# Row-paired first transform stage, full-array second stage, and a complex product summed in PSUM, in a convolution and gated-unit kernel

## The chip, the core and the metric

The kernel runs on one core of one Trainium2 chip, as one program. Its engines are TensorE (PE in the profile, with PEld for the loading of its stationary operand), VectorE (DVE), ScalarE (ACT), GpSimd (POOL) and SyncE (SP), which issues nearly all DMAs. Operands lie in the on-chip memory SBUF; matmul results go to PSUM, which here is cut into eight tiles of 128 partitions by 512 floats (eight banks). The metric is the device time of one execution in microseconds, lower is better.

## What is computed

For an input `u` of 2048 tokens by 448 channels the reference mixes two branches with a gate per token. Branch A is a diagonal state-space convolution: from 448 x 256 modes it makes a kernel of 2048 taps per channel and convolves by a Fourier transform of twice the length. Branch B is a gated linear unit with 1792 hidden units.

```python
    def _A_ref(u, log_A_real, A_imag, C_real, C_imag, log_dt, D_skip):
        ...
        P = jnp.exp((A * dt[:, None])[:, :, None] * pos[None, None, :])
        K = 2.0 * jnp.einsum("dn,dnl->dl", C, P).real
        ...
        Kf = jnp.fft.rfft(K, L2)
        Uf = jnp.fft.rfft(u_t, L2)
        y = jnp.fft.irfft(Uf * Kf[None, :, :], L2)[:, :, :L]
        ...
        return y + u * D_skip[None, None, :]

    def _B_ref(x, w_gate, w_up, w_down):
        g = jnp.einsum("bsd,df->bsf", x, w_gate)
        u = jnp.einsum("bsd,df->bsf", x, w_up)
        h = _sigmoid(g) * u
        return jnp.einsum("bsf,fd->bsd", h, w_down)

    x = A_u
    g = _sigmoid((x * gate_w).sum(-1, keepdims=True))
    a = _A_ref(x, ...)
    b = _B_ref(x, B_w_gate, B_w_up, B_w_down)
    return g * a + (1 - g) * b
```

## The kernel before, in words

**Four kinds of work.** (1) *Parameters*: phases and powers of the modes, on VectorE, ScalarE and GpSimd. (2) *Kernel generation*, 28 chunks of 16 channels (`kgen`): TensorE makes phases in the tiles `tp` (L827, L842), ScalarE takes sines and cosines, VectorE multiplies them by powers (L866, L881 to L885), and 32-column matmuls (L890) sum over the modes into `kp`; the taps collect in `ke` and go to `kd` in DRAM, one store after chunk 13 and one after chunk 27. (3) The *gated unit*: for each of 14 hidden tiles and each block of 512 tokens two sums of 11 matmuls, the gate's and the up branch's, each in a PSUM tile `gu` (L995 to L1000; weights and inputs are split into a high and a low part, and the last 64 rows of the contraction have a matmul of their own, L1000). ScalarE takes the tanh of the gate's sum (L983), VectorE multiplies by the up branch's sum (L984) and splits the result (L987), and three matmuls per tile (L1012 to L1014) add to the output in `dn`, which VectorE adds to `ob` (L1028). (4) The *transforms*.

**The transforms.** The channels are cut into two halves of 224 (`HD`). A `Chain` holds one half's data in a tile `fx` of 128 partitions by 32 columns by 224 channels, and works in place. There are four chains: `u` of both halves, whose spectra are stored to `us`, and the generated kernel of both halves. The steps:

- *Stage 1* (L442 in `stage1_pair`): the data comes as 64 rows by 32 columns; each column has its own 64 x 128 matrix (real and imaginary parts of 64 rows side by side), loaded in tiles `ft` of four matrices. A pair of columns is two plain float32 matmuls of 224 columns into one PSUM tile `fps`, which ScalarE writes back to `fx` (L369). The profile shows each float32 matmul as two records. The fourth chain (the kernel's second half) takes another way, `stage1_split`: its data is loaded twice, to both row halves; ScalarE and VectorE make a rounded and a remainder part `sp` (L426, L427), and four single-pass matmuls per pair (L432, L433) use matrices `sh` and `sl` that GpSimd's queue loads (L321).
- *Transposition*: through DRAM (`shf`) by SP's DMAs for three chains, on VectorE (L453) for the fourth.
- *Stage 2* (L471 in `spectrum_pair`): for each pair of columns four float32 matmuls with 64 output columns each, so that the column pair lies on the two partition halves, and real and imaginary parts lie side by side.
- *Product* (`product_pair`): `ua`, 229 KB of `us`, comes by DMA. VectorE forms all four real products in `ub` (L500), then two subtractions and two additions on 64 partitions each (L506, L507). One float32 matmul of 448 columns takes the inverse second stage into `fz` (L511), and ScalarE writes it back.
- *Back*: transposition again, then `back_j`: float32 matmuls with 64 output columns (L546), and VectorE adds the result, times the gate, to the gated unit's part (L550).

**What sets the order.** Every instruction is recorded with what it reads and writes, a cost and a priority. `Plan.order` is a list scheduler: it takes the engine that can start first and on it the ready instruction of the lowest priority number, with its own cost formulas (`c_mm`, `c_dve`, ...). The resulting order is fixed; on the chip each engine runs its list in order and waits on semaphores. Generation has priority 20, the `u` chains 30, the kernel's chains 40 and 41, the gated unit's matmuls 60, so those fill what the others leave. A tile from a pool needs a free buffer, and the counts are constants: `GUB` for `gu`, `FPS` for `fps`, `SX` and `SK` for the buffers of the kernel's two chains.

**PSUM before.** `gu` 3, `dn` 1, `fps` 1 and, during generation, `tp` 2 and `kp` 1: eight. After generation the latter three give way to `fps`, `fz` and `fzx` of the last stage.

## Time and profile before

| | |
|---|---|
| times of the runs | 881.62, 883.9, 888.26 us |
| median | 883.9 us |
| span of the profiled execution, first to last instruction | 878.0 us |
| mean granted TensorE clock | 0.972 |
| HBM read and written | 78.32 MB and 36.24 MB |

The profile gives the profiled execution's span, and no time of its own that includes what lies around it; the median of the runs is 5.9 us above that span.

How to read it: "busy" is the time in which at least one instruction of the engine ran. Matmuls are pipelined and their ends are modelled, so that a record's length holds some 0.2 us in which the next matmul already runs; the distance between the starts of two neighbours is what one matmul costs. A row of groups gives line, engine, operation, tile written and tiles read, form, count, then busy us and mean ns, then the engine's idle time before them and what ended it. A row of waits gives who waited for whom: us in total, times, longest.

### The profile page before, as it was taken

What the parts mean: (1) busy time and instruction counts of PE and PEld (TensorE: products, weight loads), DVE (VectorE), ACT (ScalarE), POOL (GpSimd) and SP (SyncE); (2) the same over time, 40 slices, a digit from 0 to 9 for tenths busy, and PEclk for the clock granted to TensorE, in tenths of its full rate; (3) what the DMA queues carried; (4) which work ended last, traced back from release to release, by engine and by line L of the source; (5) the groups of instructions that cost most, each with busy time, mean ns of one, the idle gap of its engine ahead of it and who ended that gap; (6) DMA issues with size and microseconds to landing.
All of it is one profiled execution on the core that took longest, in us unless ns stands there. A gap on an engine that the chain in (4) does not pass through costs nothing. (4 is left out here: it accounts for less than half of the span.)

```text
span 878.0 us, 16776 instructions
## 1 busy us (share of the span) xinstructions
PE 808.5 (92%) x6688; PEld 541.5 (62%) x6688; DVE 733.0 (83%) x982; ACT 501.3 (57%) x862; POOL 330.1 (38%) x358
## 2 busy tenths in 40 slices
PE   4988799999988999999998999999989999889987
PEld 2665576666655667776665666666766566445543
DVE  2869984798995999999897989899846788978995
ACT  3544654677766877777677987777722352221210
POOL 3367644454452645374355535645021120000000
PEclk9989999899997999999999999999999999998999
DMA  9951377222290326436494116422959953294324
GB/s 242 226 107 32 97 216 168 95 95 93 81 194 26 125 83 146 160 116 157 135 219 120 44 60 180 125 84 79 208 104 248 280 153 109 70 212 119 85 56 117
DMA packets 95831, 115.66 MB, mean 132 GB/s; under 512 B 31465, under 2 KB 80937, under 8 KB 95241
## 3 DMA queue, kind: packets, MB, share of 16 engines
q1 hardware_dynamic: 93704, 110.98, 48.4%
q0 software_dynamic: 2048, 3.61, 1.6%
q8 instruction: 53, 0.87, 0.4%
q14 instruction: 26, 0.20, 0.1%
HBM read 78.32 MB, written 36.24 MB: 130 GB/s over the span
## 5 line engine op out<-in xcount | busy, mean ns | idle before, releaser
L995 PE MATMUL gu_gps<-xs_glu,wh_glu 128*128 128x512 f32 x336 | 148.0, 440 | 11.7 <-ACT wh_glu L969 11.6
L866 DVE TENSOR_TENSOR es_eg<-tb_eg 128x512 f32<-128x512 f32 x168 | 125.5, 772 | 20.7 <-PE kp_egp L890 19.2
L997 PE MATMUL gu_gps<-xs_glu,wl_glu 128*128 128x512 f32 x336 | 135.3, 403 | 1.2 <-POOL wl_glu L971 1.2
L996 PE MATMUL gu_gps<-xs_glu,wh_glu 128*128 128x512 f32 x336 | 135.5, 403 | 0.0
L1012 PE MATMUL dn_gps<-vh_glu,hh_glu 128*128 128x448 f32 x224 | 98.6, 440 | 7.0 <-ACT ob_glu L1021 3.5
L971 POOL TENSOR_TENSOR wl_glu<-xr_glu,wh_glu 128x512 fp32r<-128x512 f32 x44 | 77.8, 1777 | 65.7 <-ACT wh_glu L969 65.7
L995 PEld LDWEIGHTS gu_gps<-xs_glu,wh_glu 128*128 128x128 f32 x336 | 65.6, 195 | 41.2 <-issue 19.0
L1013 PE MATMUL dn_gps<-vh_glu,hl_glu 128*128 128x448 f32 x224 | 83.7, 374 | 4.5 <-DVE hl_glu L987 4.5
L1014 PE MATMUL dn_gps<-vl_glu,hh_glu 128*128 128x448 f32 x224 | 83.6, 373 | 0.5 <-POOL vl_glu L971 0.5
L884 DVE TENSOR_TENSOR ec_eg<-ec_eg,es_eg 128x1024 f32<-128x1024 f32 x56 | 79.8, 1426 | 0.0
L997 PEld LDWEIGHTS gu_gps<-xs_glu,wl_glu 128*128 128x128 f32 x336 | 65.3, 194 | 18.0 <-POOL wl_glu L971 2.8
L813 POOL TENSOR_TENSOR tb_eg<-tb_eg 128x96 f32<-128x96 f32 (+2 forms) x84 | 73.4, 877 | 5.8
L827 PE MATMUL tp_egp<-pos_sb,ph_eg 96*128 96x512 f32 x168 | 72.5, 446 | 1.9 <-ACT fr_eg L845 1.7
L885 DVE TENSOR_TENSOR es_eg<-fr_eg,es_eg 128x1024 f32<-128x1024 f32 x56 | 73.3, 1310 | 0.3
L996 PEld LDWEIGHTS gu_gps<-xs_glu,wh_glu 128*128 128x128 f32 x336 | 65.8, 196 | 10.0 <-issue 1.3
L971 POOL TENSOR_TENSOR vl_glu<-vr_glu,vh_glu 128x448 fp32r<-128x448 f32 x24 | 35.5, 1477 | 87.0 <-ACT vh_glu L969 85.5
L1012 PEld LDWEIGHTS dn_gps<-vh_glu,hh_glu 128*128 128x128 f32 x224 | 42.9, 191 | 39.0 <-issue 17.1
L803 POOL MEMSET tb_eg<- 128x96 f32 x28 | 7.8, 283 | 152.0 <-DVE es_eg L866 152.0
L1028 DVE SCALAR_TENSOR_TENSOR ob_glu<-dn_gps,og,ob_glu 128x448 f32<-128x448 f32 x72 | 49.1, 681 | 18.4 <-PE dn_gps L1014 17.7
L859 ACT ACTIVATE ec_eg<-ec_eg,half_pi 128x1024 f32<-128x1024 f32 x56 | 63.9, 1140 | 0.0
L471 PE MATMUL fps_fups<-fx_fu,m_sb 128*64 128x224 f32 x384 | 48.7, 376 | 15.6 <-DMA fx_fu<-shf 7.8
L984 DVE SCALAR_TENSOR_TENSOR sg_glu<-sg_glu,gu_gps 128x512 f32<-128x512 f32 x56 | 38.1, 682 | 24.8 <-PE gu_gps L1000 18.1
(167 smaller groups left out, 1720.0 us busy)
## 6 DMA issues: line engine op xcount, KB each, us to landing
shf<-fx_fu SPq DMA_DIRECT2D x16, 896.0 KB
fx_fu<-shf SPq DMA_DIRECT2D x16, 896.0 KB
xr_glu<-in_w_dram SPq DMA_DIRECT2D x52, 256.0 KB
us<-fx_fu SPq DMA_DIRECT2D x4, 1792.0 KB
vr_glu<-in_w_dram SPq DMA_DIRECT2D x28, 224.0 KB
gt_pro<-in_u_dram SPq DMA_DIRECT2D x8, 448.0 KB
fx_fu<-in_u_dram SPq DMA_DIRECT2D x8, 448.0 KB
kd<-ke_eg SPq DMA_DIRECT2D x8, 448.0 KB
```

Of the source, the lines that this page charges most:

```text
L813: pool(96 * m, lambda n=n, m=m: G.tensor_mul(g3(n + 1, m), g3(1, m), g3(n, 1).to_broadcast([128, 32, 3, m])))
L827: T.matmul(tp.real, ph[:, c % 2, 128 * nh:128 * nh + 128].bitcast(F32R), pos[:, 512 * i:512 * i + 512], start=True, stop=last)
L866: V.tensor_mul(o.rearrange("p d (i k) -> p d i k", k=ny), x.unsqueeze(3).to_broadcast([128, 16, nx, ny]), y.unsqueeze(2).to_broadcast([128 ...
L884: op("DVE", c_dve(1024), lambda: V.tensor_mul(ec[:, :, 0:64], ec[:, :, 0:64], es[:, :, 0:64]), [es], [ec], prio)
L885: op("DVE", c_dve(1024), lambda: V.tensor_mul(es[:, :, 0:64], fr.real, es[:, :, 0:64]), [fr], [es], prio)
L971: op(eng, cost(n), lambda: e.tensor_sub(view(l), a(), view(h).bitcast(F32)), [res, (h, key)], [(l, key)], prio)
L995: T.matmul(p.real, wh[:, k, cs], x[:, k], start=(k == 0), stop=False)
L996: T.matmul(p.real, wh[:, k, cs], x[:, 4 + k], start=False, stop=False)
L997: T.matmul(p.real, wl[:, k, cs], x[:, k], start=False, stop=False)
L1012: T.matmul(p[:, :D], hh[:, ts], vh.real, start=(i == 0), stop=False)
L1013: T.matmul(p[:, :D], hl[:, ts], vh.real, start=False, stop=False)
L1014: T.matmul(p[:, :D], hh[:, ts], vl.real, start=False, stop=(i == len(fs) - 1))
```

## The change

Stage 1 of all chains works on both row halves of the array. Even columns of the data lie on partitions 0 to 63, odd ones on 64 to 127, and so do the matrices. Four columns are four float32 matmuls, which alternate between the row halves and write two PSUM tiles. `stage1_split` and its casts, `sh`, `sl` and `sp` are gone; the fourth chain loads its data once.

Stage 2 is one float32 matmul of 448 columns with the whole 128 x 128 matrix, so that real parts lie on the lower partitions and imaginary parts on the upper ones. For the product `ua` is loaded in two arrangements side by side (the real parts of `us` on both partition halves, then the imaginary parts on both), 458 KB by two DMAs. VectorE's product is one instruction as before. The four subtractions and additions are gone: the inverse is two float32 matmuls of 448 columns that accumulate in one PSUM tile, the second with a rearranged, sign-changed copy of the matrix, which widens `m_sb` to 384 columns.

The buffers: `GUB` 3 to 2, `FPS` 1 to 2; `fz` and `fzx` are gone, the first half's later steps stay in the two `fps` tiles, and the second half's chain has three `fps` tiles of its own; `ua` 3 to 2, `ub` 1 to 2. The planner can give one instruction two new tiles of one tag.

```diff
-WB, ECB, FRB, TPB, KPB, GUB, FPS, SGB, XRB = 3, 2, 2, 2, 1, 3, 1, 3, 5
+WB, ECB, FRB, TPB, KPB, GUB, FPS, SGB, XRB = 3, 2, 2, 2, 1, 2, 2, 3, 5
...
-SX = {'ft': 1, 'ua': 3, 'ub': 1, 'fps': 1, 'fz': 1}
-SK = {'ft': 2, 'sh': 2, 'sl': 2, 'sp': 3, 'ua': 3, 'ub': 1, 'fps': 1, 'fz': 1}
+SX = {'ft': 1, 'ua': 2, 'ub': 2, 'fps': 2}
+SK = {'ft': 2, 'ua': 2, 'ub': 2, 'fps': 3}
...
+    m[0:64, 256:384], m[64:128, 256:384] = m[64:128, 128:256], -m[0:64, 128:256]
...
+    s1 = s1.reshape(64, 16, 2, 128).transpose(2, 0, 1, 3).reshape(128, 16 * 128)
...
-            t = o["ready"]
+            t, n = o["ready"], {}
...
-                if q["next"] != x.idx or not q["free"]:
+                k = n[id(q)] = n.get(id(q), -1) + 1
+                if q["next"] + k != x.idx or len(q["free"]) <= k:
                     return None
-                t = max(t, min(q["free"]))
+                t = max(t, sorted(q["free"])[k])
...
-            return self.ps[k].tile(("fps", "fz" + self.suffix)[k], self.bufs[("fps", "fz")[k]], (128, 512))
+            return self.ps[k].tile("fps", self.bufs["fps"], (128, 512))
...
-        def stage1_pair(self, tb, r, l):
-            p = self.psum()
-
-            def f():
-                for i in range(2):
-                    T.matmul(p[:, i * HD:i * HD + HD], tb[0:64, l + i], self.x[0:64, 2 * r + i], start=True, stop=True)
-            op("PE", c_mm(HD, 8), f, [tb, (self.x, r)], [p], self.prio)
-            evac(lambda: self.pair(r), p, [(self.x, r)], self.prio)
+        def stage1_four(self, tb, b, l):
+            x, ps = self.x, [self.psum(), self.psum()]
+            xr = [(x, (z, r)) for z in range(2) for r in (2 * b, 2 * b + 1)]
+            def f():
+                for a in range(2):
+                    for z in range(2):
+                        rows = slice(64 * z, 64 * z + 64)
+                        T.matmul(ps[z][:, a * HD:a * HD + HD], tb[rows, l + a], x[rows, 4 * b + 2 * a + z], start=True, stop=True)
+            op("PE", 2 * c_mm(HD, 4) + 290, f, [tb, *xr], ps, self.prio)
+            for z in range(2):
+                op("Act", c_act(D), lambda z=z: S.activation(
+                    x[:, 4 * b + z:4 * b + z + 3:2], ps[z][:, :D].rearrange("p (a d) -> p a d", a=2), AF.Copy),
+                   [ps[z]], [*xr, (x, 2 * b), (x, 2 * b + 1)], self.prio)
...
-            def f():
-                for c in range(2):
-                    for i in range(2):
-                        T.matmul(p[64 * i:64 * i + 64, c * HD:c * HD + HD], m_sb[:, 64 * c:64 * c + 64],
-                                 self.x[:, 2 * r + i], start=True, stop=True)
-            op("PE", c_mm(HD, 8) + 100, f,
+            op("PE", c_mm(D, 4), lambda: T.matmul(p[:, :D], m_sb[:, 0:128], self.pair(r), start=True, stop=True),
...
-                ua = self.tile("ua", (128, 2, HD))
-                dma(lambda ua=ua, r=r: ua.real, lambda r=r: us[:, 2 * r:2 * r + 2], 128 * 2 * HD * 4,
-                    [(us, r // 8)], [ua], self.prio)
+                ua = self.tile("ua", (128, 2, 2, HD))
+                for c in range(2):
+                    dma(lambda ua=ua, c=c: ua[64 * c:64 * c + 64],
+                        lambda r=r: us.v("(c p) k d -> p c k d", c=2)[:, :, 2 * r:2 * r + 2], 64 * 4 * HD * 4,
+                        [(us, r // 8)], [(ua, c)], self.prio)
...
-            op("DVE", c_dve(2 * D), lambda: V.tensor_mul(      # Ur Kr, Ur Ki, Ui Kr, Ui Ki
-                ub.real, ua.real.unsqueeze(2).to_broadcast([128, 2, 2, HD]),
-                p[:, :D].rearrange("p (c d) -> p c d", c=2).unsqueeze(1).to_broadcast([128, 2, 2, HD])), [ua, p], [ub], prio)
-
-            def add(i):
-                rows = slice(64 * i, 64 * i + 64)
-                V.tensor_sub(x[0:64, 2 * r + i], ub[rows, 0, 0], ub[rows, 1, 1])
-                V.tensor_add(x[64:128, 2 * r + i], ub[rows, 0, 1], ub[rows, 1, 0])
-            for i in range(2):
-                op("DVE", 2 * c_dve(HD), lambda i=i: add(i), [ub], [(x, r)], prio)
+            op("DVE", c_dve(2 * D), lambda: V.tensor_mul(
+                ub.real, ua.v("p c k d -> p c (k d)"), p[:, :D].unsqueeze(1).to_broadcast([128, 2, D])), [ua, p], [ub], prio)
             z = self.psum(1)
-            op("PE", c_mm(D, 4), lambda: T.matmul(z[:, :D], m_sb[:, 128:256], self.pair(r), start=True, stop=True),
-               [(x, r), m_sb], [z], prio)
+            def f():
+                for c in range(2):
+                    T.matmul(z[:, :D], m_sb[:, 128 + 128 * c:256 + 128 * c], ub[:, c], start=c == 0, stop=c == 1)
+            op("PE", c_mm(D, 8), f, [ub, m_sb], [z], prio)
...
-    su = dict(SU, fps=1)
+    su = dict(SU, fps=FPS)
...
-    ks = [Chain(fu, fups, su, 0, P_K, K0D), Chain(fk, fkps, SK, 1, P_K + PKD, True, True)]
+    ks = [Chain(fu, fups, su, 0, P_K, K0D), Chain(fk, fkps, SK, 1, P_K + PKD, True)]
...
-            ks[h].move(fk, fkps, SX)
+            ks[h].move(fk, (fups, fups), SX)
```

60 lines of the change are left out of this document (18 added, 42 removed).

## The prediction

> **What bounds the kernel now.** I read the page's busy times first, then the windows cut at the first and last generation matmul (164.5 and 645.4 us), then the waits in the last two.
>
> ```profile
> span 878.0 us, 16776 instructions
> PE 808.5 (92%) x6688; PEld 541.5 (62%) x6688; DVE 733.0 (83%) x982; ACT 501.3 (57%) x862; POOL 330.1 (38%) x358
> 0.00:164.50 164.50, 135.42 (x485) 95.67 (x485) 120.11 (x158) 80.47 (x127) 88.30 (x67) 0.92 0.64 151
> 164.50:645.40 480.90, 462.69 (x5249) 318.53 (x5248) 433.93 (x538) 362.94 (x628) 228.17 (x272) 0.99 0.43 119
> 645.40:878.00 232.60, 210.36 (x959) 127.30 (x956) 179.00 (x287) 57.90 (x107) 13.60 (x20) 0.98 0.57 144
> ```
>
> A window's row gives its length, the busy us of PE, PEld, DVE, ACT and POOL, the granted clock, the DMA engines' share and GB/s. TensorE is the fullest engine in both long stages (96% and 90%), VectorE second (90% and 77%). The start has neither full; its parameters have their own chain, which the change leaves alone, so I give it nothing. The waits tell how the two engines hold each other:
>
> ```profile
> DVE es_eg L866 <- PE kp_egp L890: 19.2, 19, 3.0
> PE fps_fups L546 <- DMA fx_fu<-shf: 5.3, 1, 5.3
> PE fps_fups L471 <- DVE ubx_fk L500: 4.5, 3, 2.1
> PE dn_gps L1012 <- DVE ob_glu L1028: 2.6, 8, 0.7
> PE fzx_fkps L511 <- DVE fx_fu L507: 1.4, 1, 1.4
> DVE ub_fk L500 <- DMA ua_fk<-us: 7.1, 1, 7.1
> DVE ubx_fk L500 <- DMA uax_fk<-us: 5.6, 3, 2.1
> ```
>
> The first row is generation, the others the last stage. In generation VectorE waits for TensorE's sums; in the last stage TensorE waits 8.5 us for VectorE (4.5 + 2.6 + 1.4), and each waits for DMAs.
>
> **The change part by part.** The prices:
>
> ```profile
> L442 PE MATMUL fps_fups<-fx_fu,ft_fu 64*128 64x224 f32 x192 | 49.3, 377 | 5.2 <-DMA ft_fu<-in_s1t_dram 4.3 <-DMA fx_fu<-kd 0.7
> L471 PE MATMUL fps_fups<-fx_fu,m_sb 128*64 128x224 f32 x384 | 48.7, 376 | 15.6 <-DMA fx_fu<-shf 7.8 <-DVE ubx_fk L500 4.5 <-DMA ph_eg<-phd 3.2
> L471 PE MATMUL fps_fkps<-fx_fk,m_sb 128*64 128x224 f32 x128 | 15.5, 363 | 0.9 <-DVE fx_fk L453 0.9
> L506 DVE TENSOR_TENSOR fx_fu<-ubx_fk 64x224 f32<-64x224 f32 x32 | 13.0, 406 | 0.5
> L507 DVE TENSOR_TENSOR fx_fu<-ubx_fk 64x224 f32<-64x224 f32 x32 | 12.4, 387 | 0.4
> L507 DVE TENSOR_TENSOR fx_fk<-ub_fk 64x224 f32<-64x224 f32 x32 | 12.4, 387 | 0.4
> L506 DVE TENSOR_TENSOR fx_fk<-ub_fk 64x224 f32<-64x224 f32 x32 | 12.3, 383 | 0.6
> L427 DVE TENSOR_TENSOR sp_fk<-fx_fk,sp_fk 64x448 fp32r<-64x448 f32 x16 | 9.9, 622 | 3.5 <-ACT sp_fk L426 3.4
> L984 DVE SCALAR_TENSOR_TENSOR sg_glu<-sg_glu,gu_gps 128x512 f32<-128x512 f32 x56 | 38.1, 682 | 24.8 <-PE gu_gps L1000 18.1 <-ACT wh_glu L969 6.4
> 701.19 0.37 PE L432 MATMUL fps_fkps<-sp_fk,sh_fk 128*128 128x224 f32 x1
> ...
> 702.38 0.47 PE L1012 MATMUL dn_gps<-vh_glu,hh_glu 128*128 128x448 f32 x1
> 801.84 0.36 PE L1014 MATMUL dn_gps<-vl_glu,hh_glu 128*128 128x448 f32 x1
> 802.13 0.98 PE L471 MATMUL fps_fkps<-fx_fk,m_sb 128*64 128x224 f32 x8
> 803.03 0.47 PE L1012 MATMUL dn_gps<-vh_glu,hh_glu 128*128 128x448 f32 x1
> 824.26 0.20 PE dn_gps L1012
> 826.41 0.23 PE gu_gps L995
> 827.78 0.77 PE fz_fkps L511 x2
> ```
>
> *Stage 1, three chains.* A pair is four records: 49.3 us over 48 pairs, 1.03 us each. Four columns cost 2.06 now. Nothing in this trace runs two row halves at once. Its bounds: as two pairs one after the other (2.06, no gain), or as stage 2 does with two column halves: 64.2 us over 64 pairs, 1.00 us for four matmuls of the same 224 columns. I take 1.00, the row of the same shape, as all that differs is which side of the array is halved. That is 24 x 1.06 = 25 us less.
> The Trainium skill, "TensorEngine Tiling (Array Packing)", Key Properties, says that different tiles load and multiply in parallel, row tiles included; by it the sum is the one with 1.00, and without it the gain is zero. The trace agrees for column tiles (1.00 for four against 2.06); no run here shows rows.
>
> *Stage 1, fourth chain.* From 701.19 to 702.38 a pair of four single-pass matmuls takes 1.19 us; 16 pairs 19.0. Eight groups at 1.00 make 8.0 (16.5 at 2.06): 11 us less. VectorE loses L427's 9.9 us.
>
> *Stage 2.* From 802.13 to 803.03 it takes 0.90, and its predecessor L1014 0.29 (801.84 to 802.13) against the 0.20 of an undisturbed down matmul: 0.99. The new matmul has the shape of L511, 0.77: 0.22 less, 64 times, 14 us. Here the same section of the Trainium skill says that changing the tiling mode drains the array; the 0.09 of L1014 fits that, and by the rule alone the full-array form wins on both sides.
>
> *Product.* One more matmul of L511's shape, 32 x 0.77 = 24.6 us more, all in the last stage. VectorE loses L506 and L507, 50.1 us (13.0 + 12.4 + 12.4 + 12.3).
>
> So TensorE is 26 us lighter (25 + 11 + 14 - 24.6) and VectorE 60. *DMAs*: `ua` doubles, 32 x 229 KB = 7.3 MB more on SP, two issues for one, with two buffers for three. SP waits in order, so a `ua` load behind a busy buffer holds back the weights and `acc` loads after it. The fourth chain's data and matrices fall by 1.8 and about 2 MB. The last stage's 0.57 share leaves room on average; the price is between nothing and the two `ua` waits again, 12.7 us. I take nothing: a shorter VectorE turn frees `ua` earlier relative to its next use.
>
> *Where it lies.* The order of the two built programs tells what moved. Of 1232 gate and up matmuls 969 stood before generation's last matmul and 991 do now; of 672 down matmuls 483 and 489. In generation itself TensorE gets 55 and 9 more of them, for 33 and 3 fewer at the start. Generation: 46 pairs of stage 1 become 22 groups (-25.4), 33 second stages (-7.3), 55 x 0.23 + 9 x 0.20 of gated unit (+14.5): -18 us on TensorE. But VectorE, at 434 of 481 us, gets about five more instructions like L984 (+3.4), and only the 19.2 us that it waited for L890 can shrink, so the stage gains between 0 and 15. I take 6, below the middle, because VectorE's work sets its floor. Last stage: fourth chain -11, 31 second stages -6.8, products +24.6, gated unit -22 x 0.23 - 6 x 0.20 = -6.3: TensorE's work is unchanged (+0.5). What goes there are its 8.5 us of waits for VectorE, which falls from 179 to about 118 us; the wait for `shf` (5.3) stays. I take 8. Sum: 878.0 - 6 - 8 = 864 us span; with 5.9 for what lies between this span and the median, **870 us**. One bound is left out of this sum and stands below: the lost `gu` buffer, between 0 and 26.7 us, taken as 0, since the planner knows of two buffers and puts other matmuls between.
>
> **The rivals.**
>
> *1. The gated unit stalls for PSUM (slower).* With three `gu` tiles the next gate sum never needs the last product L984; with two, the next up sum does.
>
> ```profile
> 19.77 0.50 PE L1000 MATMUL gu_gps<-xs_glu,wl_glu 64*128 64x512 f32 x1
> 25.29 0.49 PE L1000 MATMUL gu_gps<-xs_glu,wl_glu 64*128 64x512 f32 x1
> 25.60 0.68 DVE L984 SCALAR_TENSOR_TENSOR sg_glu<-sg_glu,gu_gps 128x512 f32<-128x512 f32 x1
> ...
> 834.47 0.49 PE L1000 MATMUL gu_gps<-xs_glu,wl_glu 64*128 64x512 f32 x1
> 839.64 0.50 PE L1000 MATMUL gu_gps<-xs_glu,wl_glu 64*128 64x512 f32 x1
> 841.14 3.60 DVE L453 STREAM_TRANSPOSE fx_fk<-fx_fk 128x1792 f32<-128x1792 f32 x1
> 845.44 0.77 DVE L984 SCALAR_TENSOR_TENSOR sg_glu<-sg_glu,gu_gps 128x512 f32<-128x512 f32 x1
> ```
>
> The up sum was complete at 834.96, the next gate sum at 840.14, yet L984 ended at 846.21, behind the transposes: 6.1 us in which an up sum in two tiles would stand still, and everything behind it in TensorE's list. Nine of the 56 blocks were late so, first and last shown, by 0.3 to 6.3 us, 26.7 together. It decides if the list places the next sum as tightly as before: 870 + 26.7 = 897 us. Against it: VectorE's queue is shorter in the last stage. For it: generation's long VectorE instructions are untouched, and six of the nine lie there.
> The Trainium skill, "TensorEngine Tiling (Array Packing)", Gotcha 1: PSUM Pressure, says that row tiles must write different banks; so the groups of four take two `fps` tiles, and this is what took the third `gu` tile.
>
> *2. The row halves do not overlap.* Groups of four cost 2.06. Generation's TensorE sum is then +7 (14.5 - 7.3), the last stage gets 2.5 instead of 11 from the fourth chain: +8.5, which eats the 8. With half of the 7 reaching the end, 878 + 3.5 + 0.5 + 5.9 = 888 us, no change.
>
> *3. TensorE's relief passes in full.* Generation gains its 15, and in the last stage the first half's product ends early enough that the `shf` wait (5.3) and the `ua` waits fall under gated-unit work: 8.5 + 5.3, about 14. 878 - 15 - 14 + 5.9 = 855 us. Against it: VectorE's 90% in generation.
>
> **How the numbers follow.** About 1% (8.8 us) is what a measurement can tell from no change: faster is below 875.1, slower above 892.7. Forecast 0.52, its own range 859 to 881; rival 1 0.22; rival 2 0.13; rival 3 0.13. Faster: three quarters of the forecast and rival 3, 0.52 in all. Same: the rest of the forecast (0.13), rival 2 nearly whole (0.12) and half-sized stalls of rival 1 (0.05): 0.30. Slower: 0.18, nearly all rival 1. For 8 in 10 the range runs from 852, which leaves out under half of rival 3, to 899, past the centre of rival 1.
>
> **What would show it.** In the changed kernel's groups: stage 1 with 96 + 32 matmuls in about 1.0 us per four (right) or 2 us (rival 2), starts in pairs a few ns apart; stage 2 at about 0.77; two inverse matmuls at 1.5 us per pair; no VectorE rows but one product per pair. In the windows: the last generation matmul near 639 us, and a last stage near 225 us with VectorE below 125. TensorE's waits should have few rows on VectorE; rival 1 shows as rows of gate or up matmuls waiting for L984 or the tanh, 20 us and more, rival 3 as a generation stage under 470 us. The forecast is wrong if the product's VectorE instruction waits for `ua` by more than the old 12.7 us.

## The result and the profile after

The changed kernel takes **896.6 us** (median of 4, 895.9 to 898.9) against 882.8 us for the kernel before on the same chip: a ratio of **1.0149**, 95% interval 1.0102 to 1.0195. It is slower by about 1.5%, and the forecast was 870. The profiled execution has a span of 894.2 us against 878.0. The profiled execution of the kernel before is one of its faster ones (granted clock 0.972 and span 878.0 us, where 92 other executions have a mean clock of 0.964 and a median span of 880.7), so that up to 7 us (0.008 of 880) of what looks lost to the clock since can be that draw.

The first lines of the page, and then the three windows, cut as for the kernel before at the first and the last generation matmul (155.5 and 655.0 us here; length, then busy us of PE, PEld, DVE, ACT and POOL, granted clock, share of the DMA engines, GB/s):

```profile
span 894.2 us, 15983 instructions
PE 795.5 (89%) x6368; PEld 534.7 (60%) x6368; DVE 679.2 (76%) x838; ACT 492.0 (55%) x846; POOL 320.7 (36%) x342
```

```profile
0.00:155.50 155.50, 123.75 (x460) 88.20 (x463) 117.24 (x154) 76.22 (x122) 74.31 (x59) 0.92 0.61 156
155.50:655.00 499.50, 459.73 (x5108) 316.41 (x5107) 443.27 (x544) 368.22 (x638) 245.30 (x282) 0.96 0.42 118
655.00:894.20 239.20, 212.02 (x810) 130.09 (x806) 118.67 (x141) 47.61 (x87) 1.13 (x1) 0.93 0.61 151
```

TensorE is busy for 13 us less (808.5 to 795.5) and VectorE for 54 less (733.0 to 679.2), and yet generation got 18.6 us longer (480.9 to 499.5) and the last stage 6.6 (232.6 to 239.2); only the start is 9.0 shorter, with 33 gate and up matmuls fewer in it. The granted clock fell in both long stages: 0.99 to 0.96 and 0.98 to 0.93. Against the forecast, generation ends 15.6 us late (655.0 for 639.4) and the last stage is 14.6 too long (239.2 for 224.6).

The groups of the changed operations (busy us, mean ns, idle time before them):

```profile
L450 PE MATMUL fps_fups<-fx_fu,m_sb 128*128 128x448 f32 x96 | 49.3, 611 | 17.2 <-DMA fx_fu<-shf 10.6 <-DMA xr_glu<-in_w_dram 6.5
...
L487 PE MATMUL fps_fkps<-ub_fk,m_sb 128*128 128x448 f32 x64 | 27.2, 547 | 0.0
L422 PE MATMUL fps_fups<-fx_fu,ft_fu 64*128 64x224 f32 x192 | 25.9, 377 | 1.8 <-DMA ft_fu<-in_s1t_dram 1.5 <-DMA fx_fu<-kd 0.2
```

Stage 1 of the three chains is 25.9 us for 24 groups of four, 1.08 us each. One such group of the fourth chain in the timeline, behind a second stage (start, length, number of records):

```profile
700.50 0.92 PE L450 MATMUL fps_fups<-fx_fu,m_sb 128*128 128x448 f32 x2
701.34 1.03 PE L422 MATMUL fps_fkps<-fx_fk,ft_fk 64*128 64x224 f32 x8
702.30 0.47 PE L988 MATMUL dn_gps<-vh_glu,hh_glu 128*128 128x448 f32 x1
```

In the kernel before, eight such records (two pairs) took 2.06 us; here they take 1.03. The two row halves do run at once.

TensorE's waits over the whole span, those that grew most and the last transform's (us in total, times, longest):

```profile
PE dn_gps L988 <- DVE ob_glu L1004: 14.2, 10, 5.9
PE fps_fups L450 <- DMA fx_fu<-shf: 10.6, 2, 8.1
PE gu_gps L971 <- DVE sg_glu L960: 8.9, 6, 3.5
PE kp_egp L866 <- DVE ec_eg L860: 8.7, 9, 2.3
PE fps_fups L450 <- DMA xr_glu<-in_w_dram: 6.5, 1, 6.5
PE gu_gps L971 <- ACT sg_glu L959: 5.8, 4, 4.1
PE fps_fups L522 <- DMA fx_fu<-shf: 5.8, 1, 5.8
```

In the kernel before, `dn` waited 3.2 us for `ob`, `kp` 2.7 for `ec`, stage 2 7.8 for `shf`, and no `gu` matmul waited for `sg`. Here these are 14.2, 8.7, 10.6 (with 6.5 more, put down to the transfer that landed last) and 14.7 us (8.9 + 5.8). The last transform's wait for `shf` (L522) stayed, 5.8 for 5.3.

**An account that separates work from waiting.** The trace has a record of TensorE's granted clock, which is either full or one half. I count as *work* TensorE's busy time less half of what lay under half clock, so that the same matmuls count the same at either clock. Then span = work + idle + half-clock loss:

| us | work | idle | half-clock loss | span |
|---|---|---|---|---|
| before | 788.8 | 69.5 | 19.7 | 878.0 |
| after | 761.9 | 98.6 | 33.6 | 894.2 |
| difference | **-26.9** | **+29.1** | **+13.9** | +16.2 |

The forecast had TensorE's work 26 us lighter; it is 26.9. All of it, and 16 us on top, came back as time in which TensorE stood or ran at half clock. The account is good to some us only: four lists of before's arithmetic (before, `b_gu2`, `b_gu2_fps2` and `b_hop300` below) show work of 788.8, 785.3, 780.6 and 785.7 us, the less the more half clock there was, so it counts some of the half-clock loss too high.

### The profile page after: what moved, and what is told of

Same layout as the page of the kernel before. It is cut to its first block, busy times and chain, and to the rows that moved or that the text cites. A ratio compares the mean times of both kernels' runs of the same rounds, so it can differ in the third digit from the quotient of the medians.

```text
span 894.2 us, 15983 instructions
## 1 busy us (share of the span) xinstructions
PE 795.5 (89%) x6368; PEld 534.7 (60%) x6368; DVE 679.2 (76%) x838; ACT 492.0 (55%) x846; POOL 320.7 (36%) x342
## 3 DMA queue, kind: packets, MB, share of 16 engines
q1 hardware_dynamic: 102216, 117.60, 49.7%
## 4 chain that ended last, share of the span: by engine, by line
PE 43%; DVE 25%; DMA 19%; issue 4%; SPq 4%; POOL 3%; ACT 2%; DVEq 0%; POOLq 0%; ACTq 0%
DMA fx_fu<-shf 6%; DVE es_eg L842 5%; PE fps_fups L450 4%; PE kp_egp L866 4%; PE gu_gps L971 4%; SPq L321 4%; PE dn_gps L988 3%; PE gu_gps L972 3%; PE gu_gps L973 3%; DVE ec_eg L860 3%; PE tp_egp L803 3%; PE dn_gps L989 2%; PE dn_gps L990 2%; PE gu_gps L976 2%; PE fps_fups L487 2%
## 5 line engine op out<-in xcount | busy, mean ns | idle before, releaser
L842 DVE TENSOR_TENSOR es_eg<-tb_eg 128x512 f32<-128x512 f32 x168 | 135.7, 830 | 25.4 <-PE kp_egp L866 19.9
L988 PE MATMUL dn_gps<-vh_glu,hh_glu 128*128 128x448 f32 x224 | 99.7, 445 | 14.9 <-DVE ob_glu L1004 14.2
L971 PEld LDWEIGHTS gu_gps<-xs_glu,wh_glu 128*128 128x128 f32 x336 | 66.0, 197 | 54.7 <-issue 12.7
L989 PE MATMUL dn_gps<-vh_glu,hl_glu 128*128 128x448 f32 x224 | 84.4, 377 | 3.9 <-DVE hl_glu L963 3.9
L803 PE MATMUL tp_egp<-pos_sb,ph_eg 96*128 96x512 f32 x168 | 75.3, 459 | 4.3 <-DVE fr_eg L809 3.9
L789 POOL TENSOR_TENSOR tb_eg<-tb_eg 128x96 f32<-128x96 f32 (+2 forms) x84 | 76.3, 913 | 6.1
L947 POOL TENSOR_TENSOR vl_glu<-vr_glu,vh_glu 128x448 fp32r<-128x448 f32 x24 | 33.6, 1402 | 116.4 <-ACT vh_glu L945 116.3
L861 DVE TENSOR_TENSOR es_eg<-fr_eg,es_eg 128x1024 f32<-128x1024 f32 x56 | 70.3, 1256 | 0.2
L988 PEld LDWEIGHTS dn_gps<-vh_glu,hh_glu 128*128 128x128 f32 x224 | 43.5, 194 | 42.7 <-DVE ob_glu L1004 16.2
L959 ACT ACTIVATE sg_glu<-gu_gps 128x512 f32<-128x512 f32 x56 | 33.5, 598 | 63.1 <-PE gu_gps L976 61.9
L450 PE MATMUL fps_fups<-fx_fu,m_sb 128*128 128x448 f32 x96 | 49.3, 611 | 17.2 <-DMA fx_fu<-shf 10.6
L962 ACT ACTIVATE hh_glu<-sg_glu 128x512 fp32r<-128x512 f32 x56 | 34.7, 633 | 45.2 <-DVE sg_glu L960 39.5
```

The costliest lines, as they stand in the source:

```text
L450: op("PE", c_mm(D, 4), lambda: T.matmul(p[:, :D], m_sb[:, 0:128], self.pair(r), start=True, stop=True), [(self.x, r), *([] if self.on_dve ...
L789: pool(96 * m, lambda n=n, m=m: G.tensor_mul(g3(n + 1, m), g3(1, m), g3(n, 1).to_broadcast([128, 32, 3, m])))
L803: T.matmul(tp.real, ph[:, c % 2, 128 * nh:128 * nh + 128].bitcast(F32R), pos[:, 512 * i:512 * i + 512], start=True, stop=last)
L842: V.tensor_mul(o.rearrange("p d (i k) -> p d i k", k=ny), x.unsqueeze(3).to_broadcast([128, 16, nx, ny]), y.unsqueeze(2).to_broadcast([128 ...
L947: op(eng, cost(n), lambda: e.tensor_sub(view(l), a(), view(h).bitcast(F32)), [res, (h, key)], [(l, key)], prio)
L971: T.matmul(p.real, wh[:, k, cs], x[:, k], start=(k == 0), stop=False)
```

## Experiments

Each ratio is to the kernel before, timed beside it, with its 95% interval. The account of each profiled execution stands beside it; single executions of a kernel differ by up to some 10 us, so times are compared by ratio and the account says where the time lay.

The names of the theories: **P**, the lost third `gu` tile (rival 1's mechanism). **S**, the planner's fixed list reaches a second stage before its transposed data, and TensorE stands. **M**, the second inverse matmul loads the fullest engine in the last stage. **L**, any newly planned list differs by per cents. **K**, work is as summed, and the time is lost to idle and half clock because of the traded tiles. **T**, TensorE's work sets the time; **C**, chains of waits do. **E**, a tail at the end.

### The traded tiles alone, and the product alone

`b_gu2`, the kernel before with two `gu` tiles:

```
-... KPB, GUB, FPS, ... = 1, 3, 1, ...
+... KPB, GUB, FPS, ... = 1, 2, 1, ...
```

> The kernel before with two gu tiles for three, nothing else. Theory P (the lost gu tile costs the time): 893 to 910 us, 10 to 27 more than before, with TensorE waiting 15 us or more on L983 and L984 in rows of gu_gps. Theory S (TensorE's fixed list reaches stage 2 before the transposed data has landed, stands, and its clock is then halved): within 1% of before, 875 to 891, since no transform is touched. Theory M (the second inverse matmul loads the fullest engine in the last stage): as before, 878 to 888.

`b_gu2_fps2`: two `gu` and two `fups` tiles, the change's allocation beside generation, with before's arithmetic:

```
-... KPB, GUB, FPS, ... = 1, 3, 1, ...
+... KPB, GUB, FPS, ... = 1, 2, 2, ...
-    su = dict(SU, fps=1)
+    su = dict(SU, fps=FPS)
```

> The kernel before with the change's trade of PSUM tiles alone: gu 3 to 2, fps 1 to 2, all arithmetic as before. Theory P: 890 to 908 us. Theory S: 875 to 891, unless the waits for fx_fu<-shf grow by more than 5 us. Theory M: 878 to 888.

`b_prod`: full-array stage 2 and accumulated product (`spectrum_pair`, `product`, `product_pair` and the matrix of the change) in the kernel before, with one tile fewer each of `ft`, `sp` and `ua`, for want of room:

```
-SX = {'ft': 1, 'ua': 3, 'ub': 1, 'fps': 1, 'fz': 1}
-SK = {'ft': 2, 'sh': 2, 'sl': 2, 'sp': 3, 'ua': 3, 'ub': 1, 'fps': 1, 'fz': 1}
+SX = {'ft': 1, 'ua': 2, 'ub': 1, 'fps': 1, 'fz': 1}
+SK = {'ft': 1, 'sh': 2, 'sl': 2, 'sp': 2, 'ua': 2, 'ub': 1, 'fps': 1, 'fz': 1}
```

> The kernel before with the full-array second stage and the accumulated product alone; stage 1, gu 3 and fps 1 as before (ua 3 to 2 buffers of double size, ft of the second half 2 to 1 and sp 3 to 2 to make room). Theory P: 870 to 884 us, as the tile is kept and VectorE loses 50 us. Theory S: as its waits for fx_fu<-shf, about 17 us as before, so 872 to 888. Theory M: 890 or more, with a last stage over 240 us against 232.6.

`a_dma200`: the changed kernel, its planner told 200 bytes per ns for a transfer instead of 350:

```
-                wire = max(wire, fin) + o["size"] / 350.0
+                wire = max(wire, fin) + o["size"] / 200.0
```

> The changed kernel with one number of the planner altered: it counts on 200 GB/s for DMAs instead of 350, so the list puts more work of other kinds (about 34 us by row prices instead of 15 to 29) between a chain's last stage-1 matmul and its first stage 2. Theory S: waits for fx_fu<-shf in generation fall from 10.6 us to under 4, half-clock stretches from 38 us to under 25, time 875 to 888 us. Theory P: the gu waits stay, 890 to 900. Theory M: the last stage stays near 239, 890 to 900.

| | ratio | interval | work | idle | loss |
|---|---|---|---|---|---|
| `b_gu2` | 1.0124 | 1.0098 to 1.0149 | 785.3 | 83.4 | 32.2 |
| `b_gu2_fps2` | 1.0569 | 1.0525 to 1.0614 | 780.6 | 102.7 | 49.7 |
| `b_prod` | 1.0497 | 1.0460 to 1.0535 | 798.3 | 91.9 | 41.7 |
| `a_dma200` | 1.0041 | 1.0014 to 1.0068 | 761.3 | 97.2 | 31.9 |

Two `gu` tiles alone cost 1.2%, and the waits are those of rival 1. From `b_gu2`'s waits:

```profile
PE gu_gps L995 <- DVE sg_glu L984: 8.2, 6, 2.5
PE gu_gps L995 <- ACT sg_glu L983: 8.1, 4, 4.0
```

16.3 us where the kernel before had none. This is one list; what another list alone can do is below. The second `fups` tile beside them makes it 5.7%, more than any theory had expected, and the runs do not show why; from there the rest of the change wins back 4.2 points (1.0569 to 1.0149). So the trade was not free, and the arithmetic was not worthless. `b_prod` measured something else as well: its last stage stretched to 271.8 us, with TensorE waiting 18 us in the last transform (L540), whose matrices now had one tile, so it says little of the product.

`a_dma200` did to generation what S said, and its time, 888.3 us, is at the edge of S's range, 1.1 points under the change. Its windows (this execution took 892.2 us):

```profile
174.40:654.70 480.30, 453.00 (x5106) 313.20 (x5105) 441.77 (x549) 367.49 (x638) 229.92 (x271) 0.98 0.43 120
654.70:890.40 235.70, 195.44 (x731) 117.17 (x727) 110.56 (x131) 42.17 (x78) 1.16 (x1) 0.91 0.61 152
```

The `shf` waits are gone from generation, which takes 480.3 us, 19 less than in the change; but it starts 19 us later, since the planner put more of the gated unit ahead of it, and in this execution the work is that of the change and the lost time near it (129 us for 132).

### Parts on the kernel before with its three tiles, and the rest on the change

`mix` (on the kernel before): three `gu` tiles, one `fups` tile and the old stage 1 on three chains, as before; from the change the full-array stage 2, the accumulated product, and row halves in the fourth chain only, whose pool has its own tiles:

```
-SX = {'ft': 1, 'ua': 3, 'ub': 1, 'fps': 1, 'fz': 1}
-SK = {'ft': 2, 'sh': 2, 'sl': 2, 'sp': 3, 'ua': 3, 'ub': 1, 'fps': 1, 'fz': 1}
+SX = {'ft': 1, 'ua': 2, 'ub': 2, 'fps': 1, 'fz': 1}
+SK = {'ft': 2, 'ua': 2, 'ub': 2, 'fps': 2}
```

> The kernel before with its three gu tiles and one fups tile, its half-row stage 1 on the three fups chains, and from the change only the full-array stage 2, the accumulated product and the row-half stage 1 of the fourth chain (with the two tiles that this chain has of its own). TensorE's arithmetic by the measured prices: -11 - 14 + 24.6, so about 0; VectorE's -60 us. Theory P (the lost gu tile is what the change pays for, and its arithmetic is worth having): 870 to 880 us, faster than before. Theory M (the second inverse matmul loads the fullest engine where it is fullest): 885 to 895, no faster than before, although the gu tile is back, with the last stage at or above before's 232.6 us. Theory S (the planned list meets transposed data that are not there): the time goes with the half-clock time and the waits for shf, under 50 us of half clock in sum would go with a time under 880, over 80 us with a time over 890.

`a_oldprod`: the changed kernel with before's `spectrum_pair`, `product` and `product_pair`, and

```
-SX = {'ft': 1, 'ua': 2, 'ub': 2, 'fps': 2}
-SK = {'ft': 2, 'ua': 2, 'ub': 2, 'fps': 3}
+SX = {'ft': 1, 'ua': 3, 'ub': 1, 'fps': 2}
+SK = {'ft': 2, 'ua': 3, 'ub': 1, 'fps': 3}
```

> The changed kernel with the quarter-array stage 2 and VectorE's sums of the product put back: what is left of the change is the row-half stage 1 of all chains and the second fups tile for the third gu tile. Against the change TensorE is 24.6 - 14 = 10.6 us lighter, VectorE 50 us heavier. Theory M: about 886 us, faster than the change. Theory P: the trade of tiles measured 935.8 us, less the 36 us that stage 1 saves on TensorE: about 900 us, as slow as the change. A theory V, by which VectorE's relief is what the change lives on in its last stage: 905 us or more, slower than the change, the last stage over 245 us.

`b_hop300` and `a_hop300` change nothing but the planner's list:

```
-    HOP, HPE = 200.0, 260.0
+    HOP, HPE = 300.0, 360.0
```

> The kernel before with no work changed: the planner is told 300 and 360 ns instead of 200 and 260 for the way from one engine to another, which only gives another order of the same instructions. Theory L (any new list moves the time by per cents, so that the change's 1.5 per cent says little of its edits): more than 1 per cent off 883 us, in either direction. Theories P and S: within 1 per cent, 874 to 892 us.

> The changed kernel with the same two numbers of the planner changed and no work changed. Theory L: more than 1 per cent off 896.6 us, in either direction. Theory P: 888 to 905 us, since the tile is still missing. Theory S: the time follows the waits for shf in generation and the half-clock time: under 882 us if these waits go as they did with the slower planned transfers, 890 to 905 if they stay.

`b_four`: the kernel before with row halves in the fourth chain alone (`stage1_four` instead of `stage1_split`), that is `mix` with before's product and stage 2:

```
-SK = {'ft': 2, 'sh': 2, 'sl': 2, 'sp': 3, 'ua': 3, 'ub': 1, 'fps': 1, 'fz': 1}
+SK = {'ft': 2, 'ua': 3, 'ub': 1, 'fps': 2}
```

`mix_hop300` and `b_four_hop300` are these two under the other list, and `a_gu3_tp1` is the change with a third `gu` tile in place of a `tp` tile:

```
-... TPB, KPB, GUB, FPS, ... = 2, 1, 2, 2, ...
+... TPB, KPB, GUB, FPS, ... = 1, 1, 3, 2, ...
-SK = {'ft': 2, 'ua': 2, 'ub': 2, 'fps': 3}
+SK = {'ft': 2, 'ua': 2, 'ub': 2, 'fps': 2}
```

> The kernel before with one part of the change that needs no tile of the generation stage: the fourth chain's stage 1 by row halves (its own pool has the second tile once generation is over). All else, the product and stage 2 too, as before. Theory K (TensorE's work at full clock is what the sum said, and the change pays in time that TensorE stands or runs at half clock, mostly for the trade of the gu tile): work 11 us below before's 788.8, lost time as in the lists that keep three gu tiles (89 to 109 us), so a span of 867 to 887 and a median near 872 if the list is a good one. Theory M (the accumulated product is what costs in the last stage): the same sign, faster than before and at least 15 us under the kernel that has the accumulated product too (897.0). Theory L (new lists cost by themselves): anywhere within 1 per cent of before, no gain that holds under a second list.

> The kernel with three gu tiles, the accumulated product, the full-array stage 2 and the fourth chain's stage 1 by row halves, under the planner's other list (300 and 360 ns for the way between engines). Its first list measured 897.0 us with TensorE idle for 71.0 us as before, but 75.4 us of work at half clock against 39.4. Theory K with a bad draw of half-clock stretches: the work stays at 785 us, the lost time falls to about 100, span 880 to 890. Theory M (the second inverse matmul costs in the last stage whatever the list): 893 us or more again, the last stage at 239 us or more.

> The kernel before with the fourth chain's stage 1 by row halves, under the planner's other list (300 and 360 ns). Before itself went from 883 to 885.5 us under that list. Theory K: the 11 us of work are gone here too, so about 875 us, below the 885.5 of the same planner without the edit. Theory L: no closer to the first list's gain than to none, 880 to 895.

> The changed kernel with the third gu tile back and one tp tile fewer in its place (the phase products of generation then have one tile, not two; the fourth chain has two fps tiles, not three). Theory P (the lost gu tile): TensorE's lost time falls from 132 us towards 109, the time to 875 to 885 us, if one tp tile is enough. Theory K as it stands (two fups tiles beside generation cost as much as the lost gu tile): lost time stays at 120 us or more, 885 to 900 us. If the tp tile is what generation cannot spare, it is over 900 us and TensorE's waits are those of tp for fr.

| | ratio | interval | work | idle | loss |
|---|---|---|---|---|---|
| `mix` | 1.0160 | 1.0091 to 1.0230 | 785.0 | 71.0 | 37.7 |
| `mix_hop300` | 1.0129 | 1.0076 to 1.0182 | 788.6 | 79.4 | 21.3 |
| `a_oldprod` | 1.0158 | 1.0088 to 1.0229 | 756.0 | 100.6 | 29.3 |
| `b_hop300` | 1.0039 | 1.0004 to 1.0075 | 785.7 | 70.8 | 29.4 |
| `a_hop300` | 1.0104 | 1.0068 to 1.0140 | 760.0 | 95.4 | 30.5 |
| `b_four` | 0.9977 | 0.9942 to 1.0013 | 774.2 | 72.3 | 34.8 |
| `b_four_hop300` | 1.0052 | 1.0019 to 1.0085 | 773.0 | 80.5 | 29.6 |
| `a_gu3_tp1` | 1.0983 | 1.0935 to 1.1032 | 765.3 | 159.7 | 42.7 |

Three things follow. *L is half a per cent to one, not several*: another list of the same work moved the kernel before by +0.4% and the change by -0.5% (1.0149 to 1.0104, `a_dma200` -1.1%). The change's first list was its worst of three, but all three are slower than before, and all three have the same work (760 to 762) and the same idle time (95 to 99).

*P is not the whole cause.* `mix` has all three `gu` tiles and before's idle time (71.0), and is as slow as the change. From `b_four` to `mix` the steps are the full-array stage 2 and the product with its buffers, and the new list that they bring: work +10.8 us (24.6 for the second inverse less 14), span +12.3, ratio +1.8%; under the other list +0.8%. That it is the extra matmul on TensorE that costs this, as M has it, is not shown. Under the other list the last stage, where that matmul lies, is 225.9 us with the product and 230.5 without, and generation 510.7 and 497.8; `a_oldprod`, with before's product, is as slow as the change; and `a_1inv` below, without the matmul, gains 0.3% by the ratios. What is shown is that the 50 us taken off VectorE buy nothing: in the last stage VectorE's idle time is 63 us in `b_four` and 121 in `mix`. In the change's last stage the product waits 51 us for TensorE's stage 2, and in the kernel before 0.5:

```profile
DVE ub_fk L481 <- PE fps_fkps L450: 30.4, 12, 3.4
DVE ubx_fk L481 <- PE fps_fups L450: 20.6, 10, 3.1
DVE ub_fk L500 <- PE fps_fkps L471: 0.5, 2, 0.3
```

*Saved work does not come off the time.* `b_four` has 14.6 us less work than the kernel before and the same time (K had 872); by the two profiles 17.9 us more were lost. The clearest case is `a_gu3_tp1`, whose list, with one `tp` tile, put all gate and up matmuls ahead of the last generation matmul. It is 9.8% slower, outside every range but the last; the waits of `tp` for `fr` that this one named are 6.2 us, too little for the 87 by which it is slower. Its windows, and a stretch of its last stage:

```profile
154.80:754.90 600.10, 558.79 (x5488) 390.87 (x5486) 464.27 (x603) 400.36 (x673) 203.54 (x273) 0.96 0.36 101
754.90:967.70 212.80, 119.10 (x403) 54.28 (x403) 78.74 (x81) 25.84 (x50) 0.00 (x0) 0.81 0.66 162
```

```profile
853.76 0.92 PE L450 MATMUL fps_fkps<-fx_fk,m_sb 128*128 128x448 f32 x2
...
854.71 1.09 DVE L481 TENSOR_TENSOR ub_fk<-ua_fk,fps_fkps 128x896 f32<-128x896 f32 x1 [2.68 <-PE fps_fkps L450]
...
855.94 1.74 PE L487 MATMUL fps_fkps<-ub_fk,m_sb 128*128 128x448 f32 x4 [1.27 <-DVE ub_fk L481]
...
857.52 0.92 PE L450 MATMUL fps_fkps<-fx_fk,m_sb 128*128 128x448 f32 x2
```

Its last stage has about half of TensorE's busy time (119 us against 212 in the change) and not one gate or up matmul, and still takes 212.8 us: 93 us less work, at a granted clock of 0.81, for 26 us less time than in the change. A pair of the product goes from stage 2 to VectorE to the inverse, and the next pair's stage 2 stands behind that inverse in TensorE's order: one round from 853.76 to 857.52, 3.8 us, for 2.7 us of matmuls. Of the last stage some 200 us are such a sequence: it starts 35 us after the last generation matmul (the kernel's store and reload), then stage 1, 16 us of VectorE transposes, sixteen rounds, transposes, last transform. In the other lists the gated unit fills its gaps.

### The same order, with work left out

To free the comparison from the planner, these keep every instruction in its place (the planner is told the old costs) and make some shorter. `a_1inv`: the change without the second inverse matmul. `b_half1`: the kernel before with one of the two stage-1 matmuls of a pair left out in three chains. `b_noadd`: without VectorE's imaginary sum, and `b_half1_noadd` with both.

```
-                    for c in range(2):
-                        T.matmul(z[:, :D], m_sb[:, 128 + 128 * c:256 + 128 * c], ub[:, c], start=c == 0, stop=c == 1)
+                    T.matmul(z[:, :D], m_sb[:, 128:256], ub[:, 0], start=True, stop=True)
```

```
-                for i in range(2):
-                    T.matmul(p[:, i * HD:i * HD + HD], tb[0:64, l + i], self.x[0:64, 2 * r + i], start=True, stop=True)
+                T.matmul(p[:, 0:HD], tb[0:64, l], self.x[0:64, 2 * r], start=True, stop=True)
```

```
-                V.tensor_add(x[64:128, 2 * r + i], ub[rows, 0, 1], ub[rows, 1, 0])
```

> The changed kernel with the second of the two inverse matmuls of each product pair left out (the part of the sum with the other half of the array rows is missing from the output); order and tiles exactly as in the change. TensorE does 32 x 0.77 = 24.6 us less, all of it in the last stage. Theory M (TensorE's load is what the last stage waits for): 872 to 880 us. Theory C (the last stage is a chain of short steps, each waiting for the one before, with TensorE's other work beside it): only the 16 matmuls that stand in the fourth chain's own sequence count, at most 12 us, and the clock's share of it comes off: 884 to 897.

> The kernel before with one of the two stage-1 matmuls of each pair left out in the three chains that run beside the start and the generation (the other half of the pair's columns gets a copy of the first); order, tiles and every other instruction as before, three gu tiles. TensorE does 48 x 1.03 = 49 us less. Theory T (TensorE sets the time up to the last generation matmul, as the prediction had it): 835 to 850 us, the generation stage near 440. Theory C (the waits in the list set it, and TensorE's saving turns into idle and half clock): less than half of it is gained, 860 to 883.

> The kernel before with VectorE's sum for the imaginary parts left out of the product (64 instructions of 0.39 us, 25 us of VectorE's time in the last stage, the imaginary rows keep what they held); order and tiles as before. Theory T or M (TensorE binds the last stage): within 5 us of 882. Theory C: the sums stand in the sequence of a pair, 2 x 0.39 us in each of the fourth chain's 16 pairs, so 5 to 13 us faster: 869 to 878.

> Both leave-outs together in the kernel before: TensorE 49 us less, VectorE 25 us less, order and tiles as before. If the two add, the gain is the sum of the two gains; if both were held up by the same waits, it is about the larger of the two; if each had only moved the bound to the other, it is more than their sum. Theory T: 830 to 850 us. Theory C: 850 to 875.

| | left out | ratio | interval | work | idle | loss |
|---|---|---|---|---|---|---|
| `a_1inv` | TensorE 22 us | 1.0117 | 1.0070 to 1.0164 | 739.5 | 113.2 | 34.0 |
| `b_half1` | TensorE 20 us | 0.9914 | 0.9874 to 0.9954 | 769.2 | 78.0 | 27.9 |
| `b_noadd` | VectorE 25 us | 0.9945 | 0.9902 to 0.9988 | 788.3 | 63.2 | 22.4 |
| `b_half1_noadd` | both of before's | 0.9889 | 0.9855 to 0.9923 | 767.6 | 68.5 | 33.5 |

The expectations of `b_half1` and `b_half1_noadd` mis-stated its size: 1.03 us is a pair of stage-1 matmuls, so half of it is left out, 48 x 0.51 = 25 us, of which the account shows 19.6. With that size theory T has about 857 us (882 less 25) instead of 835 to 850. Its generation window against before's 480.90:

```profile
158.50:638.40 479.90, 452.62 (x5157) 304.37 (x5156) 437.90 (x539) 362.87 (x628) 230.18 (x272) 0.98 0.43 119
```

TensorE is busy there for 10 us less, and the stage is 1 us shorter (the start 6). In time, 20 us less TensorE work gives 0.9%, about 8 us (4 to 11); 22 us less in the change 0.3% by the ratios and 7 us by the medians (889.2); 25 us less VectorE work 5 us (1 to 9), and both together 10 (7 to 13), not to be told from their sum. So an engine's work, even with the order held and 92% busy, counts for a fifth to two fifths in this kernel by the middle of these ranges. T falls, and so does M's 872 to 880 for `a_1inv`; the times lie within C's ranges, of which that of `b_noadd` (869 to 878) touches T's, within 5 us of 882.

### The tail

In the change the last transform's last result is out at 874.0 us, 219.0 us after the last generation matmul; before it was 872.8, and 227.4. What follows it is longer: 20.2 us against 5.2. The timeline of that tail:

```profile
878.65 0.69 DVE L1004 SCALAR_TENSOR_TENSOR ob_glu<-dn_gps,og,ob_glu 128x448 f32<-128x448 f32 x1 [0.29 <-PE dn_gps L990]
...
879.39 0.47 PE L988 MATMUL dn_gps<-vh_glu,hh_glu 128*128 128x448 f32 x1 [0.78 <-DVE ob_glu L1004]
...
879.70 0.36 PE L989 MATMUL dn_gps<-vh_glu,hl_glu 128*128 128x448 f32 x1
...
881.14 0.71 PE L988 MATMUL dn_gps<-vh_glu,hh_glu 128*128 128x448 f32 x1 [0.87 <-DVE ob_glu L1004]
...
881.65 0.57 PE L989 MATMUL dn_gps<-vh_glu,hl_glu 128*128 128x448 f32 x1
...
883.37 0.74 PE L988 MATMUL dn_gps<-vh_glu,hh_glu 128*128 128x448 f32 x1 [0.78 <-DVE ob_glu L1004]
```

The gated unit's last down sums go one after the other through the single `dn` tile, each waiting 0.8 us for VectorE to empty it: a round is 1.75 us (879.39 to 881.14), and after a few of them the clock halves (L989 takes 0.57 instead of 0.36) and a round is 2.23 (881.14 to 883.37). `mix` (18.8 us), `a_oldprod` (20.3) and `a_hop300` (21.0) end the same way, `b_four` with 11.0. In the kernel before the last transform's matmuls stand between these sums, in rounds of about that length (870.89 to 872.53, 1.64 us):

```profile
870.05 0.60 PE L546 MATMUL fps_fkps<-fx_fk,ft_fk 128*64 128x224 f32 x4
870.89 0.47 PE L1012 MATMUL dn_gps<-vh_glu,hh_glu 128*128 128x448 f32 x1 [0.25 <-DVE ob_glu L1028]
...
871.69 0.60 PE L546 MATMUL fps_fkps<-fx_fk,ft_fk 128*64 128x224 f32 x4
872.53 0.47 PE L1012 MATMUL dn_gps<-vh_glu,hh_glu 128*128 128x448 f32 x1 [0.25 <-DVE ob_glu L1028]
```

So part of the 8.4 us is paid for in the tail: sums that stood between the transform's matmuls now stand behind them. `a_dma200` has them the other way round, a tail of 8.1 us and its last transform out after 227.5, in a last stage of 235.7.

`a_dn2` and `b_four_dn2` give every second of the last eight down sums another tile:

```
-        p = gps.tile("dn", 1, (128, 512))
+        late = H == 1 and fs == FGS[1][-1] and j % 2
+        p = fkps.tile("fps", SK["fps"], (128, 512)) if late else gps.tile("dn", 1, (128, 512))
```

> The changed kernel in which every second of the last eight down sums of the gated unit takes its PSUM tile from the fourth chain's three instead of the single dn tile; the order of TensorE's instructions is the change's but for its last 30. Theory E (a tail of down sums through one tile costs the last stage what its shorter transforms gain): the eight sums now take turns in two tiles, each bound by its three matmuls (about 0.8 us) instead of 1.64 to 2.27 us a round, so the tail falls from 20.2 to 8 to 13 us and the time by 7 to 12 us: 885 to 890. If the tail only hides another end (the stores of the result), 894 to 899.

> The kernel before with the row-half stage 1 in the fourth chain alone and the same second place for the last down sums (there they follow the last transform in a tail of 11.0 us). Theory E: the tail falls to 5 to 7 us, the time from 882.8 to 877 to 879, half a per cent under before. If before's order of instructions is simply the best that its planner's numbers give (theory L): 882 or more.

`a_dn2`: 1.0115, interval 1.0076 to 1.0154 (median 893.0); `b_four_dn2`: **0.9947**, interval 0.9922 to 0.9972 (median 877.9). In `a_dn2` the sums follow closely:

```profile
870.18 0.36 PE L991 MATMUL dn_gps<-vl_glu,hh_glu 128*128 128x448 f32 x1
...
870.38 0.36 PE L989 MATMUL fps_fkps<-vh_glu,hh_glu 128*128 128x448 f32 x1
...
875.24 0.47 PE L989 MATMUL dn_gps<-vh_glu,hh_glu 128*128 128x448 f32 x1 [1.52 <-ACT hh_glu L962]
```

0.2 us from one sum to the next, but then the last four sums wait for the last block's high part `hh`. The tail fell from 20.2 to 15.9 us and the median by 3.5, a third to a half of what theory E expected. In `b_four_dn2` the tail went from 11.0 to 8.7 and the median from 882.8 to 877.9, as E had it. Both go E's way, but against its neighbour each one's interval overlaps, so the gain of the second tile alone is not shown. `b_four_dn2` is the one version with nothing left out that beats both kernels, the kernel before by half a per cent; what else differs between two profiles of that list and its neighbour is within their scatter.

## Why the prediction was wrong

**Right: the prices of arithmetic.** Stage 1 at 1.08 us and 1.03 a group (1.00 said), VectorE's product sums gone, TensorE's work -26.9 us (-26 said), VectorE's -54 (-60). Rival 2 is refuted by the row halves' 1.03 us for eight records. The Trainium skill, "TensorEngine Tiling (Array Packing)", Key Properties, has different tiles working in parallel; for row tiles this trace now agrees (1.03 us where one row half took 2.06). Stage 2 and the inverse are 0.92 us for their two records in the timeline and 1.74 for four, where 0.77 and 1.5 were said, because a record's end overlaps the next one's start; from start to next start, at full clock, their medians are 0.75 and 1.50. The work in sum agrees within what the account can tell.

**Near in number by luck, failed in mechanism: "I take 8" in the last stage.** The last transform is out 8.4 us earlier (227.4 to 219.0 us). But what was to go there, TensorE's waits for VectorE, did not: all rows of that kind are 12.1 us before (the three of the sum among them) and 11.6 after, although VectorE did fall to 118.7. The largest after:

```profile
PE dn_gps L988 <- DVE ob_glu L1004: 4.8, 6, 0.9
PE gu_gps L971 <- DVE sg_glu L960: 3.5, 1, 3.5
PE fps_fups L487 <- DVE ubx_fk L481: 2.6, 2, 2.0
```

VectorE's relief became waits of its own for stage 2, the 51 us shown above. **Failed: that the stage ends with the transforms.** The forecast of 225 us missed the tail behind them, +15.0, of which no step of the sum spoke. It could be asked of the trace of before: what fills TensorE between the last transform's matmuls, and where does it go if these come earlier.

**Failed, and the larger error: "I take 6" in generation and the lost `gu` buffer "taken as 0, since the planner knows of two buffers and puts other matmuls between".** The last generation matmul moved from 645.4 to 655.0 instead of to 639. The planner did know of the buffer, and still the two tiles alone cost 1.2% (`b_gu2`, 16.3 us of waits), inside the bounds of 0 to 26.7 that the text gave and far from the 0 that it chose. The second `fups` tile beside it raised that to 5.7%. The sum also had no term for a list that reaches stage 2 before its data: the change waits 10.6 us for `shf` there, and 6.5 put down to another transfer, and `a_dma200`, without these waits, is at 1.0041. The Trainium skill, "TensorEngine Tiling (Array Packing)", Gotcha 1: PSUM Pressure, warns that row tiling raises the need for PSUM; 1.2% and 5.7% are what giving up the tile cost here, with before's arithmetic.

**Failed: the step from work to time.** The sum turned 6 of the 18 us that generation's TensorE was to lose into time. With the order held that share is about what the kernel before gives (4 to 11 us for 20); the change gives a third or less (3 to 7 us for 22). But the order is not held: planned anew, 14.6 us less work gave nothing (`b_four`), and in the change generation grew by 18.6 us with 3 us less TensorE time in it (462.7 to 459.7, where -18 was said), at a granted clock of 0.96 instead of 0.99. A stage 96% busy does not say that its work sets its length: the list is made to fill it, and less work leaves holes.

**The term of 5.9 us** for what lies between the span and the median was mostly the distance of before's profiled execution from its median: each execution of the change lasts 1.7 to 1.8 us longer than its span, and its median lies 2.4 above the profiled one.

**Rival 1** named 897 us, and the time is 896.6, but that is partly luck: of its mechanism `gu` waits of 14.7 us are in the trace where it had 26.7, and without the trade `mix` is as slow. **Rival 3**, a generation under 470 us, is refuted (499.5). The price of nothing for `ua` held: the product's VectorE instruction waits 7.5 us for it in the changed last stage, 12.7 before.

**What stays open.** How the 1.5% divides. By the way before, `b_four`, `mix`, after, the steps are -0.2%, +1.8%, -0.1%; by the way before, `a_oldprod`, after, they are +1.6% and -0.1%. The trade with its row halves and the product each cost some 1.5% when first made and nothing when made second, within intervals of half a per cent or more, and another list alone moves the change by as much as 1.1; the profiles show the waits that each brings, but no run shows why they do not add. Three `gu` tiles with two `fups` tiles and two `tp` was not tried, since there is no ninth PSUM bank, nor row halves that share one tile.

## What to carry to other kernels

Before an engine's saved work is counted as time, ask which sequence sets the end of the stage and what the work stood between: an engine at 90% that a planner keeps full by filling gaps gave back a fifth to two fifths here, and a buffer taken from it can cost more than the instructions saved. To price an edit apart from the new order it causes, leave the work out with the order held. Where a fixed list ends, look at what is left running alone: a serial tail through one PSUM tile can eat what the stage ahead of it gained.

## What was not expected of the hardware

A short stand of TensorE is mostly followed by a stretch at half clock, and so costs more than itself. I take the stands in all 20 traces that begin at full clock, after the first 20 us, and ask whether a half-clock stretch begins between the stand's start and 5 us after its end: so it is for 111 of 112 stands of 3 us or more, 69 of 85 of 2 to 3 us, 33 of 54 of 1.5 to 2 us, and 22 of 123 of 1 to 1.5 us. From any moment at full clock such a stretch begins within 7 us in 11% of cases. 28 of the 256 stretches had no stand of 1 us in the 5 us before them, and no run here changes the stands alone, so this is a count and not a cause. A stretch is 3.4 us or a multiple of it, most often 3.4 to 10.2, where the end of the kernel does not cut it off. The stand for `shf` at 222.3 us in the change, in the chain of waits:

```profile
211.38 18.79 DMA fx_fu<-shf
230.41 3.32 PE fps_fups L450 x4
```

The four second-stage records after it take 3.32 us, where two take 0.92 at full clock; the half-clock stretch there lasts 10.2 us. The Trainium skill, "TensorE: Matmul & The Clock Gate", in "HAM oscillation — how this bites in real kernels", gives gaps over about 3.4 us as what to avoid; here most stands of 2 to 3 us (69 of 85) already had a half-clock stretch behind them. By the account such stretches cost 33.6 us of the changed kernel's span, 13.9 more than before, half of the work that it saved.
